# The row-maximum pass of pooled-query attention on full-height TensorE tiles

## The chip, the cores and the metric

The kernel runs on one core of a Trainium2 chip. The metric is the device time of one execution in microseconds; a run of the kernel before is given as the median of its executions. A profile of one execution shows what each engine did: TensorE (PE, with its weight loads as PEld), VectorE (DVE), ScalarE (ACT), GpSimd (POOL) and SyncE (SP), which issues all transfers here.

## The reference

The computation is an attention over 8 batches and 8 heads, with keys and values of 1152 rows of 64, whose queries are the means of neighbouring rows (576 per head), followed by a feed-forward block with g = h cos(h). The shapes of the feed-forward block are 4608 x 512 times 512 x 2048, and 2048 x 512 back.

```python
q_pool = q.reshape(B, H, S // 2, 2, D).mean(axis=3)
scores = scale * np.matmul(q_pool, k.transpose(0, 1, 3, 2))
scores = scores - np.max(scores, axis=-1, keepdims=True)
attn = np.exp(scores)
attn = attn / (np.sum(attn, axis=-1, keepdims=True) + 1e-09)
x = np.matmul(attn, v)            # then heads side by side: (4608, 512)
h = x @ w_in
out = (h * np.cos(h)) @ w_out
```

## The kernel before

**Precision.** Every f32 operand that is multiplied is split into a high and a low f16 half, and products are summed from three f16 matmuls. `q1T` holds the high half of the pooled queries, transposed and stacked twice (64 + 64 partitions); `k1` holds, per head, the high half of the keys in one half of the partitions and the low half in the other. `q2T` and `k2` hold the low half of the queries together with the row maxima, so that the score matmuls subtract the maximum by themselves.

**Pairs and units.** Two heads of a batch make a pair; there are 32 pairs. The 576 pooled queries of a head are four tiles of 128 and a remainder of 64; the remainders of the two heads share one slot (`2 * QT`) of the query tiles, head 0 in the first 64 rows and head 1 in the other. The main loop walks over 32 x 9 units: scores (`s_unit`, line 875, and `s_rem`, line 895), exponentials and their split into halves (`soft`, lines 921 to 930), the products with the values (`av`, line 945), and a share of the feed-forward block of an earlier batch (`ffn1`, line 1190, `ffn2`, line 1246).

**The row-maximum pass.** Before the exponentials of a pair, the pass finds the maximum of every score row. It is spread over the units of the two pairs ahead by the table `JOBS`, and each group writes a two-bank tile `mx` (one buffer, for the first pair alternating with `st`), from which VectorE takes the maxima:

- `mx_main` (line 670): eight groups per pair (four query tiles, two key chunks), each of two matmuls, one per head, of 64 contraction rows, 128 output rows and 512 columns;
- `mx_rest` (line 687, in the profile 688): one group of eight matmuls of 128 columns for the last 128 keys;
- `mx_mixed` (line 710): one group of four matmuls for the remainders, on 64 x 64 tiles, 512 columns;
- `mx_mixed_rest` (line 727): one group of two such matmuls of 128 columns.

The head's half of the partitions, `HALF[h]`, selects the tile rows, so the pass multiplies high halves with high halves only.

**Preparing the queries.** `pool_q` adds neighbouring rows on POOL, `prep_q1` writes the f16 copy twice into `q1s` (ScalarE for the first four pairs, VectorE behind them), `transpose_q1` transposes it by a DMA on SP's queue into `q1T`, and `prep_q2` forms the low half on POOL. `q1s` is a tile of a pool with one buffer.

**The order of work.** All instructions are recorded first, then `arrange` puts them into an order for each engine: a list schedule with a cost for each instruction, in which the earliest possible start wins. Its costs for TensorE are 0.421 ns per output column, nothing for a matmul on the lower half of a tile of 64 rows, and 0.1 us where the tile height changes:

```python
            if size[0] == 64 and tuple(i.tile_position)[0] == 64:
                c = 0.0
...
        if e == "PE" and nd["tile"] != mode:
            c += 0.1
            mode = nd["tile"]
```

The order within an engine is then fixed; semaphores hold an instruction back until its inputs are there.

Of the kernel before, what the change touches and what calls it, by code (L numbers as in the profile page):

```python
# [10 lines left out]
F16 = mybir.dt.float16  # L11
# [8 lines left out]
P = 128  # L20
# [19 lines left out]
NDIR = 4  # L40
# [277 lines left out]
def tile_attention_ffn(  # L318
# [9 lines left out]
    nc = tc.nc  # L328
    B, H, S, D = q.shape
# [11 lines left out]
    KT = S // P  # L341
    QT = SQ // P
# [8 lines left out]
    NSL = 2 * QT + 1  # L351
    RB = 512 // P
    JR = 2 * RB
    HALF = (slice(0, D), slice(D, P))

    fix = ctx.enter_context(tc.tile_pool(name="fix", bufs=1))
    sb1 = ctx.enter_context(tc.tile_pool(name="sb1", bufs=1))
# [4 lines left out]
    k2 = [fix.tile([P, KT, 2, P], F16, name=f"k2_{i}") for i in range(2)]  # L362
    qs2 = fix.tile([P, NSL, P], F16, name="qs2")
    nc.gpsimd.memset(qs2, 0.0)
    vc = [fix.tile([P, 2, KT, 2 * D + 2], F16, name=f"vc_{i}") for i in range(2)]
    vf = [t.bitcast(F32) for t in vc]
    for i in range(2):
# [193 lines left out]
    def after(ins, prev):  # L561
        if prev is not None:
            extra.append((ins.ins.name, prev.ins.name))
        return ins

    k1 = [fix.tile([P, KT, 2, P], F16, name=f"k1_{i}") for i in range(3)]
    kst, kld, qld, q1T, q2T, vld, vam, mxs = {}, {}, {}, {}, {}, {}, {}, {}
# [42 lines left out]

    def prep_q1(n):
        qs = qld[n][:, :, 0, :]
        q1s = sb1.tile([P, NSL, 2, D], F16, tag="q1s", name="q1s")
        src = qs.unsqueeze(2).broadcast_to([P, NSL, 2, D])
        if n < NDIR:
            nc.scalar.copy(q1s, src)
        else:
            nc.vector.tensor_copy(q1s, src)
        qld[n] = qs, q1s

    def transpose_q1(n):
        q1s = qld[n][1]
        t = sb1.tile([P, NSL, P], F16, tag="q1T", bufs=3, name="q1T")
        tr = nc.sync.dma_start_transpose(t, q1s.rearrange("p s a d -> p (s a d)"))
        if gate[0] is None:
            gate[0] = tr
        q1T[n] = t

    def prep_q2(n):
        qs, q1s = qld.pop(n)  # L630
        v4 = qs2[:, 0 : 2 * QT].rearrange("p (t h) (a d) -> p t (h a) d", h=2, a=2)
        nc.gpsimd.tensor_sub(
            v4[:, :, 0::3, :],
            qs[:, 0 : 2 * QT].rearrange("p (t h) d -> p t h d", h=2),
            q1s[:, 0 : 2 * QT, 0, :].rearrange("p (t h) d -> p t h d", h=2),
        )
        for h in range(2):
            nc.gpsimd.tensor_sub(
                qs2[HALF[h], 2 * QT, HALF[h]],
                qs[HALF[h], 2 * QT],  # L640
                q1s[HALF[h], 2 * QT, 0],
            )

    def transpose_k(n, js):
# [13 lines left out]
    def mx_tile(n):  # L658
        mx_n[0] += 1
        tag = "st" if n == 0 and mx_n[0] % 2 else "mx"  # L660
        return psum.tile([P, 2, 512], F32, tag=tag, name=tag)

    def mx_main(n, t, c):
        if n not in mxs:
            mxs[n] = sb2.tile([P, NSL, 3], F32, tag="mxs", name="mxs")
        m = mx_tile(n)
        last = None
        for h in range(2):
            last = after(
                nc.tensor.matmul(  # L670
                    m[:, h, :],
                    q1T[n][HALF[h], 2 * t + h, :],
                    k1[n % 3][HALF[h], c * RB : (c + 1) * RB, h, :],
                    start=True,
                    stop=True,
                    skip_group_check=True,
                ),
                last,
            )
        nc.vector.reduce_max(mxs[n][:, 2 * t : 2 * t + 2, c], m, axis=AX.X)  # L680

    def mx_rest(n):
        m = mx_tile(n)
        last = None
        for t in range(QT):
            for h in range(2):
                last = after(
                    nc.tensor.matmul(
                        m[:, h, t * P : (t + 1) * P],
                        q1T[n][HALF[h], 2 * t + h, :],  # L690
                        k1[n % 3][HALF[h], KT - 1, h, :],
                        start=True,
                        stop=True,
                        skip_group_check=True,
                    ),
                    last,
                )
        nc.vector.reduce_max(
            mxs[n][:, 0 : 2 * QT, 2].rearrange("p (t h) -> p h t", h=2),
            m.rearrange("p h (t c) -> p h t c", c=P),  # L700
            axis=AX.X,
        )

    def mx_mixed(n):
        m = mx_tile(n)
        last = None
        for c in range(2):
            for h in range(2):
                last = after(
                    nc.tensor.matmul(  # L710
                        m[HALF[h], (c + h) % 2, :],
                        q1T[n][HALF[h], 2 * QT, HALF[h]],
                        k1[n % 3][HALF[h], c * RB : (c + 1) * RB, h, :],
                        start=True,
                        stop=True,
                        skip_group_check=True,
                    ),
                    last,
                )
        nc.vector.reduce_max(mxs[n][:, 2 * QT, 0:2], m, axis=AX.X)  # L720

    def mx_mixed_rest(n):
        m = mx_tile(n)
        last = None
        for h in range(2):
            last = after(
                nc.tensor.matmul(
                    m[HALF[h], 0, 0:P],
                    q1T[n][HALF[h], 2 * QT, HALF[h]],
                    k1[n % 3][HALF[h], KT - 1, h, :],  # L730
                    start=True,
                    stop=True,
                    skip_group_check=True,
                ),
                last,
            )
        nc.vector.reduce_max(mxs[n][:, 2 * QT, 2:3], m[:, 0, 0:P], axis=AX.X)
# [78 lines left out]
    def mains(c, ts):  # L816
        def fn(n):
            for t in ts:
                mx_main(n, t, c)

        return fn
# [6 lines left out]
        (-2, 1, lambda n: transpose_k(n, J0)),  # L828
        (-2, 2, lambda n: load_k(n, J1)),
        (-2, 2, prep_q1),  # L830
        (-2, 2, transpose_q1),
        (-2, 3, lambda n: prep_k(n, J1)),
        (-2, 3, lambda n: transpose_k(n, J1)),
# [3 lines left out]
        (-2, 6, mains(0, (2,))),  # L837
        (-2, 7, mains(0, (3,))),
        (-2, 7, prep_q2),
        (-2, 8, mains(1, (0,))),  # L840
        (-2, 8, load_v),
# [3 lines left out]
        (-1, 0, v_max_begin),  # L845
        (-1, 1, mains(1, (3,))),
        (-1, 2, mx_rest),
        (-1, 2, mx_mixed),
        (-1, 3, mx_mixed_rest),
        (-1, 3, m_write),  # L850
        (-1, 4, transpose_q2),
# [13 lines left out]
    def s_unit(u):  # L865
        if u >= NP * NU:
            return
        p, i = divmod(u, NU)
        ka, kb, qa, qb = k1[p % 3], k2[p % 2], q1T[p], q2T[p]
        if i > 0:  # L870
            j = i - 1
            s = psum.tile([P, 2, 512], F32, tag="st", name="st")
            for h in range(2):
                for w, x, part in ((ka, qa, 0), (kb, qb, 1)):
                    nc.tensor.matmul(  # L875
                        s[:, h, :].rearrange("p (t c) -> p t c", c=P),
                        w[:, j, h, :],
                        x[:, h : 2 * QT : 2, :],
                        start=part == 0,
                        stop=part == 1,  # L880
                        skip_group_check=True,
                    )
            st[u] = [(s.rearrange("p a c -> p (a c)"), 2 * 512)]
            return
        st[u] = [s_rem(p, 0, JR, "st")]

    def s_rem(p, j0, j1, tag):
        ka, kb, qa, qb = k1[p % 3], k2[p % 2], q1T[p], q2T[p]
        s = psum.tile([P, 2, 512], F32, tag=tag, name=tag)
        for j in range(j0, j1):  # L890
            r = j - j0
            for h in range(2):
                for w, x, part in ((ka, qa, 0), (kb, qb, 1)):
                    o = (r % RB) * P + h * D
                    nc.tensor.matmul(  # L895
                        s[:, r // RB, o : o + D],
                        w[:, j, h, :],
                        x[:, 2 * QT, HALF[h]],
                        start=r % RB == 0 and h == 0 and part == 0,
                        stop=False,  # L900
                        skip_group_check=True,
                    )
        n = (j1 - j0) * P
        return s.rearrange("p a c -> p (a c)")[:, 0:n], n
# [478 lines left out]
    for u in range(NUNITS):  # L1383
# [10 lines left out]
        while credit > 0.0:  # L1394
            c = next(ffn, None)
# [47 lines left out]
```

## Time and profile before

| | us |
|---|---|
| three runs, median (lowest to highest) | 1680.79 (1677.89 to 1682.36) |
| profiled execution, span from first to last instruction | 1669.1 |
| profiled execution, own time | not given apart from the span |
| TensorE busy in it | 1554.3 |
| ScalarE busy | 1216.6 |
| VectorE busy | 1141.3 |
| POOL busy | 888.7 |

A busy time is the union of an engine's recorded instructions. Matmuls are pipelined: a matmul starts before the record of the one ahead ends, so recorded lengths add up to more than the time that TensorE spends, and the distance between starts is what a matmul costs in a stream. A shape like `64*128 64x512` names the part of the array in use (rows * columns), and then partitions x elements of the moving operand. The granted clock is the share of TensorE's full clock. The first row-maximum matmul starts at 17.1 us and the last at 1447.1 us; from 1517 us on the core works on the rest of the feed-forward block alone.

### The profile page before, as it was taken

The numbers are of one execution on the slowest core, as the hardware profiler recorded it, in microseconds if no ns is written. First come the engines' busy times: TensorE is split into PE (matmuls) and PEld (weight loads), VectorE is DVE, ScalarE is ACT, GpSimd is POOL, SyncE is SP. The second block draws the span as 40 slices with busy tenths as digits, with TensorE's granted clock in tenths as the row PEclk, the third lists the DMA queues.
The fourth block names the chain that finished last, engine by engine and source line by source line (L and its number), as shares of the span: only waits on it lengthen the run. The fifth ranks groups of instructions, "written<-read, shape, count | busy, mean of one in ns | idle before, by whom it ended". The sixth has DMA issues, their size and how long they took to land. (4 is left out here: it accounts for less than half of the span.)

```text
span 1669.1 us, 40505 instructions
## 1 busy us (share of the span) xinstructions
PE 1554.3 (93%) x17080; PEld 1015.9 (61%) x17080; DVE 1141.3 (68%) x1630; ACT 1216.6 (73%) x1476; POOL 888.7 (53%) x765
## 2 busy tenths in 40 slices
PE   3899998998899989998999999999999999997998
PEld 1577776665666566654666566665666566665664
DVE  6799896777667777766866577776678767632342
ACT  2346468887788779886987597988798879884442
POOL 3334255566566755665465556665665665461222
PEclk9899999999999999998999999999999999998999
DMA  9876853336415453444444225335434343101000
GB/s 222 188 175 137 154 103 64 79 87 111 93 49 123 79 108 67 102 79 84 90 86 97 69 51 114 65 88 98 104 78 101 63 109 52 28 21 27 14 26 19
DMA packets 336566, 146.31 MB, mean 88 GB/s; under 512 B 243712, under 2 KB 319488, under 8 KB 336384
## 3 DMA queue, kind: packets, MB, share of 16 engines
q1 hardware_dynamic: 336384, 143.73, 41.1%
q8 instruction: 133, 2.18, 0.6%
q14 instruction: 49, 0.40, 0.1%
HBM read 76.55 MB, written 10.50 MB: 52 GB/s over the span
## 5 line engine op out<-in xcount | busy, mean ns | idle before, releaser
L930 POOL TENSOR_TENSOR pp<-e,pp 128x512 f16<-128x512 f32 x374 | 445.9, 1214 | 298.8 <-ACT pp L924 126.3
L1190 PE MATMUL f<-xT,w 128*128 128x256 f16 x3456 | 416.8, 277 | 12.7 <-DVE y L1216 8.4
L921 ACT ACTIVATE e<-st,eb 128x1024 f32<-128x1024 f32 x280 | 311.1, 1111 | 137.9 <-PE st L875 100.4
L680 DVE TENSOR_REDUCE mxs<-mx 128x2 f32<-128x1024 f32 x252 | 307.5, 1220 | 151.2 <-PE mx L670 150.0
L1246 PE MATMUL f<-w,g 128*128 128x512 f16 x1728 | 395.6, 379 | 0.0
L1190 PEld LDWEIGHTS <-w 128*128 128x128 f16 x3456 | 331.6, 99 | 86.3 <-issue 37.3
L924 ACT CAST pp<-e 128x1024 f16<-128x1024 f32 x280 | 292.5, 1045 | 8.1
L945 PEld LDWEIGHTS <-pp 128*128 128x128 f16 (+1 forms) x7392 | 243.1, 100 | 76.4 <-POOL pp L930 22.7
L1246 PEld LDWEIGHTS <-g 128*128 128x128 f16 x1728 | 160.7, 98 | 192.7 <-issue 13.8
L1155 POOL TENSOR_TENSOR g<-hsc,g 128x512 f16<-128x512 f32 x144 | 188.9, 1337 | 154.8 <-ACT g L1154 145.8
L945 PE MATMUL ava<-vc,pp 128*128 128x64 f16 (+4 forms) x4784 | 249.8, 203 | 17.8 <-POOL pp L930 16.4
L875 PE MATMUL st<-q1T,k 128*128 128x512 f16 x576 | 223.0, 387 | 14.9 <-ACT e L921 14.1
L875 PE MATMUL st<-q2T,k 128*128 128x512 f16 x576 | 223.0, 387 | 0.0
L945 PE MATMUL avb<-vc,pp 128*128 128x65 f16 (+1 forms) x3312 | 206.8, 201 | 3.0 <-POOL pp L930 3.0
L1216 DVE SCALAR_TENSOR_TENSOR y<-f,r1a,y 128x512 f32<-128x512 f32 x144 | 106.9, 746 | 108.7 <-ACT y L1215 108.5
L875 PEld LDWEIGHTS <-k 128*128 128x128 f16 x1152 | 101.2, 99 | 101.9 <-issue 25.6
L1212 ACT ACTIVATE hsc<-f,r 128x512 f32<-128x512 f32 x144 | 98.3, 683 | 75.7 <-PE f L1190 74.0
L1145 DVE TENSOR_TENSOR hsc<-hsc,y 128x512 f32<-128x512 f32 x144 | 130.0, 951 | 34.2 <-ACT y L1139 33.7
L926 DVE TENSOR_TENSOR pp<-e,pp 128x1024 f16<-128x1024 f32 x93 | 128.5, 1381 | 35.3 <-ACT pp L924 34.5
L603 POOL TENSOR_TENSOR kst<-kld,kst 128x512 f16<-128x512 f32 x64 | 89.3, 1396 | 100.8 <-ACT kst L602 84.8
L670 PE MATMUL mx<-k,q1T 64*128 64x512 f16 x504 | 102.0, 401 | 33.3 <-DVE mxs L680 11.9
L670 PEld LDWEIGHTS <-q1T 64*128 64x128 f16 x512 | 26.1, 93 | 131.1 <-issue 102.8
(117 smaller groups left out, 1641.2 us busy)
## 6 DMA issues: line engine op xcount, KB each, us to landing
vld<-in_v_dram SPq DMA_DIRECT2D x32, 576.0 KB, 4.1
qld<-in_q_dram SPq DMA_DIRECT2D x64, 256.0 KB, 3.4
kld<-in_k_dram SPq DMA_DIRECT2D x32, 320.0 KB, 3.9
kld<-in_k_dram SPq DMA_DIRECT2D x32, 256.0 KB, 3.8
wraw<-in_moe_w_in_dram SPq DMA_DIRECT2D x8, 1024.0 KB, 6.5
wraw<-in_moe_w_out_dram SPq DMA_DIRECT2D x8, 1024.0 KB, 7.1
out_dram<-ob SPq DMA_DIRECT2D x32, 256.0 KB, 2.4
k<-k SPq DMA_DIRECT2D x64, 80.0 KB, 3.2
```

What stands on the lines that cost most here:

```text
L670: nc.tensor.matmul(m[:, h, :], q1T[n][HALF[h], 2 * t + h, :], k1[n % 3][HALF[h], c * RB : (c + 1) * RB, h, :], start=True, stop=True, skip ...
L680: nc.vector.reduce_max(mxs[n][:, 2 * t : 2 * t + 2, c], m, axis=AX.X)
L875: nc.tensor.matmul(s[:, h, :].rearrange("p (t c) -> p t c", c=P), w[:, j, h, :], x[:, h : 2 * QT : 2, :], start=part == 0, stop=part == 1, ...
L921: nc.scalar.activation(e, s, AF.Exp, scale=exp_scale, bias=eb)
L924: nc.scalar.copy(pp[:, 0], e)
L926: nc.vector.tensor_sub(pp[:, 1], e, pp[:, 0])
L930: nc.gpsimd.tensor_sub(pp[:, 1, c], e[:, c], pp[:, 0, c])
L945: mm = nc.tensor.matmul(out, w, x, start=start, stop=False, skip_group_check=True)
L1145: nc.vector.tensor_mul(hj, hj, y[:, j : j + 2])
L1155: nc.gpsimd.tensor_sub(gt[:, 1], hj, gt[:, 0])
L1190: mm = nc.tensor.matmul(ps[:, fi, :], w1[wt][:, hp, fs], ck.xT[hp][:, xi, cs], start=n == 0, stop=n == 3 * HP - 1, skip_group_check=True,)
L1246: nc.tensor.matmul(po, gt[:, gi, f % 2, ts_], w2[wt][:, f, :], start=f == 0 and (gi, wt) == (0, 0), stop=f == NF - 1 and (gi, wt) == (1, 0),)
```

## The change

The groups of the row-maximum pass use all 128 contraction rows. For the main and rest groups the same `q1T` slot (the query stacked twice) is multiplied by the whole `k1` slice, so that high and low halves of the keys are summed. For the remainders, the shared slot is split in two: slot `2 * QT` holds head 0's rows with zeros in the other 64, slot `2 * QT + 1` holds head 1's, and the two matmuls of a chunk are summed in one bank. `q1s` becomes a fixed tile of ten slots, of which the last two are zeroed once by POOL; `prep_q1` writes it in three copies (eight slots, then one half slot per head). `q1T` has ten slots, `s_rem` reads head 1's remainder from the last, and the transpose covers ten blocks. The scratch reserved for software-generated transfers is set to 1024 bytes. The reductions, the counts of matmuls and the job table stay.

```diff
+    q1s = fix.tile([P, NSL + 1, 2, D], F16, name="q1s")
+    nc.gpsimd.memset(q1s[:, 2 * QT :], 0.0)
...
     def prep_q1(n):
         qs = qld[n][:, :, 0, :]
-        q1s = sb1.tile([P, NSL, 2, D], F16, tag="q1s", name="q1s")
-        src = qs.unsqueeze(2).broadcast_to([P, NSL, 2, D])
-        if n < NDIR:
-            nc.scalar.copy(q1s, src)
-        else:
-            nc.vector.tensor_copy(q1s, src)
-        qld[n] = qs, q1s
+        parts = [(slice(0, P), slice(0, 2 * QT), slice(0, 2 * QT))]
+        for h in range(2):
+            parts.append((HALF[h], slice(2 * QT, NSL), slice(2 * QT + h, 2 * QT + h + 1)))
+        for ps, a, b in parts:
+            src = qs[ps, a]
+            src = src.unsqueeze(2).broadcast_to([src.shape[0], src.shape[1], 2, D])
+            if n < NDIR:
+                nc.scalar.copy(q1s[ps, b], src)
+            else:
+                nc.vector.tensor_copy(q1s[ps, b], src)
+        qld[n] = qs
...
-        t = sb1.tile([P, NSL, P], F16, tag="q1T", bufs=3, name="q1T")
+        t = sb1.tile([P, NSL + 1, P], F16, tag="q1T", bufs=3, name="q1T")
...
-                q1s[HALF[h], 2 * QT, 0],
+                q1s[HALF[h], 2 * QT + h, 0],
...
                     m[:, h, :],
-                    q1T[n][HALF[h], 2 * t + h, :],
-                    k1[n % 3][HALF[h], c * RB : (c + 1) * RB, h, :],
+                    q1T[n][:, 2 * t + h, :],
+                    k1[n % 3][:, c * RB : (c + 1) * RB, h, :],
...
                         m[:, h, t * P : (t + 1) * P],
-                        q1T[n][HALF[h], 2 * t + h, :],
-                        k1[n % 3][HALF[h], KT - 1, h, :],
+                        q1T[n][:, 2 * t + h, :],
+                        k1[n % 3][:, KT - 1, h, :],
...
-                        m[HALF[h], (c + h) % 2, :],
-                        q1T[n][HALF[h], 2 * QT, HALF[h]],
-                        k1[n % 3][HALF[h], c * RB : (c + 1) * RB, h, :],
-                        start=True,
-                        stop=True,
+                        m[:, c, :],
+                        q1T[n][:, 2 * QT + h, :],
+                        k1[n % 3][:, c * RB : (c + 1) * RB, h, :],
+                        start=h == 0,
+                        stop=h == 1,
...
-                    m[HALF[h], 0, 0:P],
-                    q1T[n][HALF[h], 2 * QT, HALF[h]],
-                    k1[n % 3][HALF[h], KT - 1, h, :],
-                    start=True,
-                    stop=True,
+                    m[:, 0, 0:P],
+                    q1T[n][:, 2 * QT + h, :],
+                    k1[n % 3][:, KT - 1, h, :],
+                    start=h == 0,
+                    stop=h == 1,
...
-                        x[:, 2 * QT, HALF[h]],
+                        x[:, 2 * QT + (h if part == 0 else 0), HALF[h]],
...
+        "TRN2", target_bir_lowering=False, num_devices=1, dynamic_dma_scratch_size=1024
```

More of the change, by code (lines that the diff above doesn't have):

```diff
@@ L612, in prep_q1 @@
         qs = qld[n][:, :, 0, :]
-        q1s = sb1.tile([P, NSL, 2, D], F16, tag="q1s", name="q1s")
-        src = qs.unsqueeze(2).broadcast_to([P, NSL, 2, D])
-        if n < NDIR:
-            nc.scalar.copy(q1s, src)
-        else:
-            nc.vector.tensor_copy(q1s, src)
-        qld[n] = qs, q1s
+        parts = [(slice(0, P), slice(0, 2 * QT), slice(0, 2 * QT))]
[9 more added lines that the diff above has]
+        qld[n] = qs
     def transpose_q1(n):
-        q1s = qld[n][1]
-        t = sb1.tile([P, NSL, P], F16, tag="q1T", bufs=3, name="q1T")
+        t = sb1.tile([P, NSL + 1, P], F16, tag="q1T", bufs=3, name="q1T")
         tr = nc.sync.dma_start_transpose(t, q1s.rearrange("p s a d -> p (s a d)"))
@@ L629, in prep_q2 @@
     def prep_q2(n):
-        qs, q1s = qld.pop(n)
+        qs = qld.pop(n)
         v4 = qs2[:, 0 : 2 * QT].rearrange("p (t h) (a d) -> p t (h a) d", h=2, a=2)
@@ L1422 @@
     from concourse.bass_utils import run_bass_kernel_spmd as _run
-    nc = _bacc.Bacc("TRN2", target_bir_lowering=False, num_devices=1)
+    nc = _bacc.Bacc(
+        "TRN2", target_bir_lowering=False, num_devices=1, dynamic_dma_scratch_size=1024
+    )
     arrays, args = {}, []
```

## The prediction

> **What bounds the kernel now.** I read the page's engine table first, then the table by stretches of the span, then the waits of TensorE, and last the timeline around single groups of the row-maximum pass.
>
> ```profile
> span 1669.1 us, 40505 instructions
> PE 1554.3 (93%) x17080; PEld 1015.9 (61%) x17080; DVE 1141.3 (68%) x1630; ACT 1216.6 (73%) x1476; POOL 888.7 (53%) x765
> 60.00:200.00 140.00, 131.52 (x1114) 100.63 (x1113) 119.85 (x198) 73.02 (x82) 51.58 (x33) 0.92 0.76 165
> 600.00:800.00 200.00, 190.06 (x2271) 121.76 (x2270) 146.65 (x212) 163.08 (x197) 121.09 (x108) 0.97 0.44 92
> 1200.00:1450.00 250.00, 245.88 (x2945) 157.28 (x2943) 183.67 (x270) 215.09 (x260) 151.78 (x134) 1.00 0.36 73
> PE st L670 <- DMA q1T<-q1s: 17.1, 1, 17.1
> PE ava L945 <- POOL pp L930: 16.4, 9, 6.9
> PE st L875 <- ACT e L921: 14.1, 12, 4.7
> PE mx L670 <- DVE mxs L680: 11.9, 11, 4.0
> ```
>
> In the stretches the columns are: length, then busy time of PE, PEld, DVE, ACT and POOL, then the granted clock. TensorE is busy 93% of the span; from 60 to 1450 us, where the row-maximum pass runs, it is idle 8.5 us of 140, 9.9 of 200 and 4.1 of 250 in the three rows shown. No other engine is above 87% in these rows. So TensorE's own stream sets the time, and the question is how much of that stream a row-maximum group takes before and after. Its busy time cannot answer that, because the recorded durations of pipelined matmuls overlap. I use starts: from the moment at which the matmul before the group has streamed out to the start of the first matmul behind the group.
>
> **The change part by part.** First the four kinds of group, at full clock. The timeline's columns are start, length, line, tiles, and count.
>
> ```profile
> 898.32 0.38 PE L875 MATMUL st<-q1T,k 128*128 128x512 f16 x1
> 898.54 0.38 PE L875 MATMUL st<-q2T,k 128*128 128x512 f16 x1
> 898.85 0.39 PE L670 MATMUL mx<-k,q1T 64*128 64x512 f16 x2
> 899.17 1.48 PE L1190 MATMUL f<-xT,w 128*128 128x256 f16 x12
> 900.49 0.41 PE L945 MATMUL ava<-vc,pp 128*128 128x65 f16 x8
> 900.74 0.41 PE L945 MATMUL avb<-vc,pp 128*128 128x65 f16 x8
> ...
> 923.61 2.75 PE L1246 MATMUL f<-w,g 128*128 128x512 f16 x12
> 926.30 0.39 PE L670 MATMUL mx<-k,q1T 64*128 64x512 f16 x2
> 926.62 5.35 PE L1246 MATMUL f<-w,g 128*128 128x512 f16 x24
> 931.81 1.47 PE L1190 MATMUL f<-xT,w 128*128 128x256 f16 x12
> ...
> 934.85 0.38 PE L875 MATMUL st<-q2T,k 128*128 128x512 f16 x1
> 935.16 0.40 PE L688 MATMUL mx<-k,q1T 64*128 64x128 f16 x8
> 935.49 1.49 PE L1190 MATMUL f<-xT,w 128*128 128x256 f16 x12
> 936.82 0.41 PE L945 MATMUL ava<-vc,pp 128*128 128x65 f16 x8
> 937.15 0.62 PE L710 MATMUL mx<-k,q1T 64*64 64x512 f16 x4
> 937.71 0.42 PE L945 MATMUL avb<-vc,pp 128*128 128x65 f16 x8
> ...
> 939.07 1.47 PE L1190 MATMUL f<-xT,w 128*128 128x256 f16 x12
> 940.47 0.24 PE L727 MATMUL mx<-k,q1T 64*64 64x128 f16 x2
> 940.65 1.49 PE L1190 MATMUL f<-xT,w 128*128 128x256 f16 x12
> ```
>
> Prices of a full-height matmul: 24 of 512 columns take 926.62 to 931.81, 0.216 us each; 12 of 256 columns take 899.17 to 900.49, 0.110 each; 8 of 64 or 65 columns take 900.49 to 900.74, 0.031 each. No f16 matmul of 128 columns on full height stands in the trace: its bounds are 0.031 and 0.110, and a straight line between them gives 0.057, which I take because the price runs nearly with the columns (0.110 to 0.216 from 256 to 512).
>
> Main groups (two matmuls of 64x512, eight groups per pair of heads). The matmul at 898.54 has streamed out at 898.756; the next stranger starts at 899.17: 0.414 us. The group behind the twelve of line 1246 gives 926.62 less (923.61 + 12 x 0.216), again 0.42. The two matmuls share the stretch (one row for both, 0.39 long, where two in turn would show 0.6), so it is one pass of 0.216 and 0.1 of dead time on either side. The neighbouring full-height kinds pass into one another without a gap (898.32 to 898.54, 900.49 to 900.74), so I put the dead time down to the change of tile size. After: 2 x 0.216 = 0.432 without dead time, **+0.018 per group**.
>
> Rest groups (eight of 64x128, one per pair): 935.49 less 935.066 is 0.424. After: 8 x 0.057 = 0.456, **+0.03** (bounds 0.25 to 0.88, so -0.18 to +0.46).
>
> Mixed groups (four of 64x512 on 64x64 tiles, one per pair): 937.71 less (936.82 + 8 x 0.031) is 0.64. After: four full passes, 0.864, **+0.22**. This is the dear one: the two diagonal tiles ran side by side, and now half of every pass multiplies zeros.
>
> Mixed rests (two of 64x128): 940.65 less (939.07 + 12 x 0.110) is 0.26. After: 2 x 0.057 = 0.114, **-0.15**: here two switches go and almost nothing comes.
>
> ```profile
> L670 PE MATMUL mx<-k,q1T 64*128 64x512 f16 x504 | 102.0, 401 | 33.3 <-DVE mxs L680 11.9 <-ACT es L921 7.8 <-ACT pps L916 7.6
> L688 PE MATMUL mx<-k,q1T 64*128 64x128 f16 x248 | 12.8, 224 | 2.5 <-DVE mxs L680 2.4
> L710 PE MATMUL mx<-k,q1T 64*64 64x512 f16 x128 | 21.1, 409 | 2.5 <-DVE mxs L698 2.0 <-DVE mxs L680 0.5
> L727 PE MATMUL mx<-k,q1T 64*64 64x128 f16 x62 | 7.5, 239 | 0.3 <-DVE mxs L720 0.2
> 949.16 0.58 PE L875 MATMUL st<-q1T,k 128*128 128x512 f16 x1 [2.95 <-ACT e L921]
> ...
> 950.39 0.63 PE L875 MATMUL st<-q2T,k 128*128 128x512 f16 x1
> 950.95 0.61 PE L670 MATMUL mx<-k,q1T 64*128 64x512 f16 x2
> 951.50 4.61 PE L1190 MATMUL f<-xT,w 128*128 128x256 f16 x24
> ```
>
> The counts give 32 pairs (128 mixed matmuls by four). For the 31 pairs behind the first: 248 x 0.018 = 4.5; 31 x 0.03 = 1.0; 31 x 0.22 = 6.8; 31 x -0.15 = -4.7. Together +7.6 us. In a half-clock stretch (matmuls of 512 columns 0.43 apart) a main group takes 0.68 (951.50 less 950.82) and would take 0.864, +0.18; with a granted clock of 0.92 to 1.00 that is some six groups, +1.0.
>
> [...]
>
> Query preparation (lines 611 to 619). One copy of 1152 elements becomes one of 1024 and two of 128.
>
> ```profile
> L618 DVE CAST q1s<-qld 128x1152 f16<-128x1152 f32 x28 | 37.7, 1345 | 32.5 <-POOL qld L609 32.4
> L924 ACT CAST pps<-es 128x128 f16<-128x128 f32 x28 | 8.3, 298 | 0.9
> 9.66 1.15 ACT L616 CAST q1s<-qld 128x1152 f16<-128x1152 f32 x1 [5.29 <-POOL qld L609]
> 10.84 1.32 SPq L624 DMA_TRANSPOSE q1T<-q1s  x1
> ```
>
> On VectorE: 1024/1152 of 1.345 is 1.20, plus 2 x 0.298 (the nearest row of that size, ScalarE's cast) is 1.79, so +0.45 for each of 28 pairs, 13 us of busy time on an engine with 528 us idle. I cost it at nothing: what waits for it is the transpose, and TensorE uses that one two units later. If the cover went, the bound is TensorE's 11.9 us of waits for reductions growing by 0.45 at each of its 11, +5. On ScalarE the first four pairs have 1.02 + 2 x 0.298 for 1.15, +0.47; for the first pair that delays TensorE's start at 17.1, which waits for this transpose. The transpose on SP's queue grows from nine blocks to ten: a ninth of the 1.32 us that its issue takes, +0.15; the loads queued behind it on SP move by as much and have units of slack. The startup thus gives +0.6; the first pairs' groups, paced there by the reductions, may add up to 11 x 0.2. I take +1 for the startup together.
>
> Priced at nothing: the memset of 256 elements (POOL's first wait, for ScalarE, outlasts it; uncovered, well under a microsecond); the column of the extra slot in lines 895 to 898 (same count and shapes); the smaller DMA scratch (the page's queues are the hardware and instruction ones; no row shows POOL issuing a transfer); the reductions, unchanged, though each starts up to 0.12 us later behind the longer group. The order of instructions is recomputed: the planner's cost of a main group goes from 0.416 with its two switches to 0.431, of a mixed one from 0.63 to 0.86, of a mixed rest from 0.25 to 0.11. These differ as the measured ones do, so the plan stays about as good, but its details will move.
>
> Cover: the added time falls partly into waits that TensorE has anyway, 22.5 us of the 590 in the three stretches, 3.8%. Bounds are nothing and all of it; I take a fifth off, since the waits are few and the extra is spread evenly: -2. Sum: 7.6 + 1.0 + 1.0 - 2 = **+7.6 us**. The profiled span would go from 1669.1 to about 1676.7. The page gives no time of its own for that execution beyond the span; the median of the runs, 1680.79, lies 11.7 above it, and I leave that margin alone: **1688.4 us**. A change of 0.3%, 5.0 us, is about what a measurement can tell from none.
>
> **The rivals.**
>
> Cover wins: the waits for POOL, ScalarE and reductions take up most of the extra, and their ends do not move. For it speaks that 3.8% of these 1390 us is some 53 us of waits, seven times the extra; against it, that POOL and ScalarE's work itself hangs on TensorE's scores and moves back with them. It leaves +0 to +5, about 1683.
>
> Faster, by stalls that the new order avoids. TensorE's longest single waits are 6.9 us for line 930's subtractions and 4.7 for line 921's exponentials, and the row at 949.16 shows what follows one of 2.95: the row of 24 matmuls of line 1190 then lasts 4.61 us in place of some 2.8, and with the matmuls between, about 3 us are lost to the half clock. The two longest gone would be -6.9 - 4.7 - 2 x 3 = -17.6, and with the +7.6 about 1671; one gone leaves the time about equal. It decides from two. Against it: nothing in the change aims at these waits.
>
> The same dice the other way: one new stall of that kind, about 1698.
>
> Narrow matmuls held up by their weight loads. If a matmul of 128 columns with a load of its own goes at the price of 256 columns, 0.110, the rest groups cost another 8 x 0.053 and the mixed rests 2 x 0.053: 31 x 0.53 is +16, 1705. Against it: matmuls of 64 columns with loads of their own run at 0.031. [...]
>
> The change does not do what it says: the dead time belongs to the change of operands, not of tile size, and stays. Then every group keeps 0.2 us: 341 x 0.2 = +68, 1756. The gapless passing of full-height kinds speaks against it.
>
> **How the numbers follow.** Forecast, slower by 5 to 11 us (1686 to 1692): 0.47. Cover wins, within 5 us: 0.28. Stalls avoided, faster: 0.16. A new stall: 0.06. Narrow matmuls: 0.02. Dead time stays: 0.01. So faster 0.16, same 0.28, slower 0.56. The range from 1675 to 1698 holds the forecast, the cover case, the small end of the avoided stalls and the new stall's centre; left out are most of the avoided stalls and the last two.
>
> **What would show it.** Main groups of two rows starting 0.216 apart, with no gap ahead and behind; mixed groups at 0.86; rest groups at 0.45; the mixed rest at 0.11; TensorE's idle time between 60 and 1450 us within some 10 us of now. It would be wrong if a gap of 0.1 us still stood at the groups' edges, if 128-column matmuls took more than 0.06, or if the long waits for lines 930 and 921 came in another number.

## The result, and the profile after

The changed kernel takes 1700.6 us (median) against 1679.34 for the kernel before on the same chip: ratio 1.0129, 95% interval 1.0104 to 1.0153, 21.3 us slower. The forecast was 1688.4, in a range of 1675 to 1698. The direction is right, the size is almost three times the forecast, and the time lies above the range. On a second chip the ratio is 1.0103 (1.0063 to 1.0143), 1710.6 against 1689.1. All times here are of undisturbed executions; one slow execution each of e4, of e12 and of the kernel before on the chip of e1 (2590 to 5050 us) is left out of the medians.

First the profile's page of the changed kernel (span, busy time of each engine), then, in its timeline, the four kinds of group. Line 675 is the main group, 693 the rest, 715 the mixed group, 732 the mixed rest.

```profile
span 1698.6 us, 40564 instructions
...
PE 1570.6 (92%) x17080; PEld 1070.4 (63%) x17080; DVE 1175.2 (69%) x1686; ACT 1217.3 (72%) x1484; POOL 903.5 (53%) x766
```

```profile
739.10 0.19 PE L900 MATMUL st<-q2T,k 128*128 128x64 f16 x1
739.12 0.59 PE L675 MATMUL mx<-k,q1T 128*128 128x512 f16 x2
739.56 2.78 PE L1195 MATMUL f<-xT,w 128*128 128x256 f16 x24
...
960.83 0.38 PE L880 MATMUL st<-q2T,k 128*128 128x512 f16 x1
961.05 0.61 PE L693 MATMUL mx<-k,q1T 128*128 128x128 f16 x8
961.50 1.47 PE L1195 MATMUL f<-xT,w 128*128 128x256 f16 x12
962.80 0.41 PE L950 MATMUL ava<-vc,pp 128*128 128x65 f16 x8
963.05 1.02 PE L715 MATMUL mx<-k,q1T 128*128 128x512 f16 x4
963.91 0.41 PE L950 MATMUL avb<-vc,pp 128*128 128x65 f16 x8
...
965.27 1.47 PE L1195 MATMUL f<-xT,w 128*128 128x256 f16 x12
966.58 0.27 PE L732 MATMUL mx<-k,q1T 128*128 128x128 f16 x2
966.69 1.47 PE L1195 MATMUL f<-xT,w 128*128 128x256 f16 x12
```

No group has a gap at its edges any more where it is shown: the main group starts 0.02 us behind a matmul of 64 columns and takes 739.12 to 739.56, 0.44; the rest 0.45, the mixed group 0.86, the mixed rest 0.11. So the price of each group is what was forecast, and the missing time is elsewhere. What changed beyond the forecast is VectorE's queue, at the copies of `prep_q1` (line 624). First the groups of that line, then one place in the timeline: VectorE, POOL and TensorE around a late copy, and the same three copies where POOL is idle.

```profile
L624 DVE CAST q1s<-qld 64x128 f16<-64x128 f32 x56 | 40.1, 715 | 0.9
...
L624 DVE CAST q1s<-qld 128x1024 f16<-128x1024 f32 x28 | 34.8, 1241 | 34.4 <-POOL qld L611 34.4
```

```profile
206.21 1.07 DVE L624 CAST q1s<-qld 128x1024 f16<-128x1024 f32 x3
...
643.29 4.95 POOL L935 TENSOR_TENSOR pp<-e,pp 128x512 f16<-128x512 f32 x4
...
643.37 3.85 DVE L624 CAST q1s<-qld 128x1024 f16<-128x1024 f32 x3 [6.35 <-POOL qld L611]
...
647.25 3.35 DVE L1150 TENSOR_TENSOR hsc<-hsc,y 128x512 f32<-128x512 f32 x4
...
650.51 1.22 DVE L685 TENSOR_REDUCE mxs<-mx 128x2 f32<-128x1024 f32 x1
...
651.78 0.21 PE L900 MATMUL mx<-q1T,k 128*128 128x64 f16 x1 [5.41 <-DVE mxs L685]
```

The three copies take 1.07 us together when POOL does nothing, and 3.85 beside POOL's subtractions. Per pair they average 2.67 (1.241 and twice 0.715). The single copy of nine slots of the kernel before took 1.345 on average, with 1.335 to 1.353 as extremes, wherever it stood; 20 of the 28 began beside a POOL instruction. So the new copies are a faster form that waits for POOL. Of the 28 large ones, 11 began while no POOL instruction ran and took 0.68 to 0.69; 17 began beside one, took 1.24 to 1.89, and each ended 0.55 behind that instruction's end. Of the 56 small ones, the 25 that began without POOL took 0.21 to 0.23; the 31 that began beside it took 0.38 to 1.42, and each ended 0.08 to 0.09 behind it. VectorE works its queue in the planned order; at 643.37 the copies had come late (6.35 us of waiting for POOL's sum of the queries), and behind them stood the products of line 1150 and the reduction that frees the `mx` buffer. TensorE waited 5.41 us for that buffer. Of this wait at most 2.5 us (3.85 less 1.345) can be the new copies': waiting for POOL's sum is as long in the kernel before, 32.4 us in all against 34.4 here.

### The profile page after: what moved, and what is told of

It is laid out like the page before. It is cut to its first block, busy times and chain, and to the rows that moved or that the text cites. A ratio compares the mean times of both kernels' runs of the same rounds, so it can differ in the third digit from the quotient of the medians.

```text
span 1698.6 us, 40564 instructions
## 1 busy us (share of the span) xinstructions
PE 1570.6 (92%) x17080; PEld 1070.4 (63%) x17080; DVE 1175.2 (69%) x1686; ACT 1217.3 (72%) x1484; POOL 903.5 (53%) x766
## 4 chain that ended last, share of the span: by engine, by line
PE 69%; DVE 10%; DMA 8%; ACT 6%; issue 3%; POOL 3%; SPq 2%; POOLq 0%; ACTq 0%; DVEq 0%
PE f L1251 20%; PE f L1195 16%; PE st L880 11%; PE ava L950 6%; PE avb L950 5%; PE mx L675 5%; DMA qld<-in_q_dram 4%; DVE mxs L685 2%; DVE q1s L624 2%; ACT e L926 2%; PE avb L1019 2%; PE mx L715 1%; DMA k<-kst 1%; POOL pp L935 1%; DMA xT<-xs 1%
## 5 line engine op out<-in xcount | busy, mean ns | idle before, releaser
L935 POOL TENSOR_TENSOR pp<-e,pp 128x512 f16<-128x512 f32 x374 | 453.2, 1234 | 303.9 <-ACT pp L929 155.2
L1195 PEld LDWEIGHTS <-w 128*128 128x128 f16 x3456 | 340.7, 99 | 88.8 <-issue 17.9
L950 PEld LDWEIGHTS <-pp 128*128 128x128 f16 (+1 forms) x7392 | 247.4, 100 | 69.0 <-POOL pp L935 14.5
L1251 PEld LDWEIGHTS <-g 128*128 128x128 f16 x1728 | 166.9, 98 | 193.0 <-issue 3.8
L1160 POOL TENSOR_TENSOR g<-hsc,g 128x512 f16<-128x512 f32 x144 | 194.3, 1374 | 148.5 <-ACT g L1159 140.9
L950 PE MATMUL ava<-vc,pp 128*128 128x64 f16 (+4 forms) x4784 | 245.1, 200 | 12.3 <-POOL pp L935 9.2
L675 PE MATMUL mx<-k,q1T 128*128 128x512 f16 x504 | 157.3, 395 | 25.3 <-DVE mxs L685 9.4
L931 DVE TENSOR_TENSOR pp<-e,pp 128x1024 f16<-128x1024 f32 x93 | 134.0, 1440 | 35.1 <-ACT pp L929 34.0
L675 PEld LDWEIGHTS <-q1T 128*128 128x128 f16 x512 | 47.9, 102 | 92.9 <-issue 36.0
```

The source lines that it names most:

```text
L675: nc.tensor.matmul(m[:, h, :], q1T[n][:, 2 * t + h, :], k1[n % 3][:, c * RB : (c + 1) * RB, h, :], start=True, stop=True, skip_group_check ...
L931: nc.vector.tensor_sub(pp[:, 1], e, pp[:, 0])
L935: nc.gpsimd.tensor_sub(pp[:, 1, c], e[:, c], pp[:, 0, c])
L950: mm = nc.tensor.matmul(out, w, x, start=start, stop=False, skip_group_check=True)
L1160: nc.gpsimd.tensor_sub(gt[:, 1], hj, gt[:, 0])
L1195: mm = nc.tensor.matmul(ps[:, fi, :], w1[wt][:, hp, fs], ck.xT[hp][:, xi, cs], start=n == 0, stop=n == 3 * HP - 1, skip_group_check=True,)
```

## The experiments

Every kernel was timed against the kernel before on its own chip (the medians of that one there: 1689 to 1693), so ratios are compared; where it matters, the kernels compared ran on one chip. Differences in us are between medians. The lines of code are shortened to what a switch does. Three switches describe nearly all of them. **Matmuls**: half height as before, or full. **Copies into `q1s`**: the single one of nine slots; the three of the change; or the same three made by reductions over one element, which give the same values:

```diff
-                nc.vector.tensor_copy(q1s[ps, b], src)
+                nc.vector.tensor_reduce(q1s[ps, b], src.unsqueeze(4), axis=AX.X, op=ALU.max)
```

**Order**: that of the changed kernel ("new"), or that of the kernel before ("old"), got by giving the planner the other kernel's costs for the row-maximum groups, the copies, the memset and the transpose:

```diff
+            if PLAN != "own" and i.name in REC:
+                as64 = PLAN == "before"
+                c = 0.0 if as64 and REC[i.name][1] else n_out(wr) * 0.000421
```

| run | matmuls | into q1s | order | median us | ratio (95%) |
|---|---|---|---|---|---|
| e1 | half | three copies | new | 1706.3 | 1.0095 (1.0068 to 1.0123) |
| e2 | full | three copies | nearly old | 1715.6 | 1.0167 (1.0140 to 1.0194) |
| e3 | full | three reductions | new | 1692.2 | 1.0018 (0.9992 to 1.0044) |
| e4 | half | three copies | nearly old | 1710.8 | 1.0130 (1.0096 to 1.0163) |
| e5 | full | three copies (the change) | new | 1710.6 | 1.0103 (1.0063 to 1.0143) |
| e6 | full | large copied, small reduced | new | 1698.2 | 1.0039 (1.0019 to 1.0058) |
| e7 | full | large reduced, small copied | new | 1707.9 | 1.0098 (1.0066 to 1.0130) |
| e9 | half | three reductions | nearly old | 1701.5 | 1.0059 (1.0032 to 1.0085) |
| e10 | full | three reductions | nearly old | 1706.6 | 1.0085 (1.0057 to 1.0113) |
| e11 | half, mixed rest full | three reductions | nearly old | 1697.5 | 1.0037 (1.0017 to 1.0058) |
| e12 | half | two copies | nearly old | 1705.1 | 1.0075 (1.0049 to 1.0102) |
| e13 | half | three reductions | old | 1706.3 | 1.0082 (1.0054 to 1.0110) |
| e14 | full | three reductions | old | 1705.3 | 1.0086 (1.0056 to 1.0116) |
| e15 | full | three copies | old | 1728.2 | 1.0221 (1.0185 to 1.0256) |
| e16 | half | two copies | old | 1706.8 | 1.0086 (1.0054 to 1.0118) |
| e17 | half | single copy, a reduction behind it | old | 1694.1 | 1.0012 (0.9991 to 1.0032) |
| e18 | half | single copy, on ScalarE | its own | 1675.6 | 0.9888 (0.9867 to 0.9909) |

e1 to e4 ran on one chip, e5 to e8 on a second, e9 to e12 on a third, e13 to e18 on a fourth. In the traces every engine of e1, e3, e5, e6 and e7 works in the order of the changed kernel, and in e13 to e17 in that of the kernel before, POOL's one memset aside.

**One part undone (e1 to e4).**

> The changed kernel with one thing undone: all matmuls of the row-maximum pass are again on 64-row and 64x64 tiles; the query preparation in three copies, the ten-slot transpose and the order of every engine stay those of the changed kernel. Kernel before 1679, changed kernel 1701. Theory PRICE (the full-height groups themselves cost some 8 us of TensorE time, the rest of the 21 us is something else): 1692 to 1694. Rival ALL-PE (the full-height matmuls cost all 21 us): 1680. Rival NOTHING (the matmuls are free, order and copies cost it all): 1700.

> The changed kernel, with the planner told the costs of the kernel before for the row-maximum groups, the query copies and the transpose, so that nearly every engine runs its instructions in the order of the kernel before. Theory PORT (the three copies into q1s run in a form that waits for POOL and stall VectorE's queue, in any order): 1697 to 1701. Rival ORDER (the new order is worse by some 13 us, the copies cost little): 1687 to 1689.

> The changed kernel in its own order, the three copies into q1s on VectorE replaced by maxima over one element, which give the same values. Theory PORT (a reduction does not wait for POOL, and each of the small ones takes about 0.3 us and not up to 1.2): 1688 to 1691, and the waits of TensorE for the mx buffer behind the reductions fall from 20 us to under 8. Rival ORDER: 1699 to 1701, waits as before.

> The kernel before in nearly its own order, with only the query preparation changed: three copies into the ten-slot q1s and a ten-block transpose. Theory PORT: 1689 to 1693. Rival ORDER: 1679 to 1682.

Taking the full-height matmuls away leaves most of the loss (e1, +17 us); taking the copies' waiting away leaves almost none of it (e3, +3 us, not told from nothing). The order of the kernel before does not rescue the change (e2, +27), and the copies alone slow the half-height kernel by 22 us there (e4). The expected times were reckoned from 1679, the kernel before on this chip takes 1689; counted from the kernel before, e1 lies between PRICE (+13 to +15) and NOTHING (+21), and e2, e3 and e4 all lie on PORT's side of ORDER. But none of the three is inside PORT's range: e2 +27 for +18 to +22, e3 +3 for +9 to +12, e4 +22 for +10 to +14. So PORT gives the direction and not the size. One detail of e3 missed too: the waits for the `mx` buffer were to fall from 20 us to under 8, and measured 16.4 in its profile. The rows of the kernel before, the changed kernel and e3 (us in total, times, longest):

```profile
PE mx L895 <- DVE mxs L680: 2.8, 2, 1.5
...
PE mx L900 <- DVE mxs L685: 20.1, 7, 5.4
...
PE mx L940 <- DVE mxs L725: 16.4, 7, 5.1
```

That wait belongs mostly to the new order, not to the copies; between the profiles of e5 and e3 no single kind of TensorE's waits differs by more than 4 us, so the gain is spread.

**Which copy (e5 to e8).** e6 and e7 replace the small ones or the large one by reductions; e8 is the kernel before, profiled again.

> The changed kernel once more, for a comparison on the same chip as the next two. Both theories: 1.3% slower than the kernel before, as it was.

> The changed kernel in its own order; only the two 64-row copies of each pair into q1s are made by VectorE reductions over one element, the copy of 1024 elements stays. Theory PORT-SMALL (the two small copies, 0.715 us each in the changed kernel against 0.28 for a reduction of their size, wait for POOL and hold VectorE's queue): most of the gain of replacing all three, 10 to 15 us below the changed kernel. Rival PORT-BIG (the copy of 1024, 0.68 us alone and up to 1.65 beside POOL, does it, mainly by blocking POOL): within 4 us of the changed kernel.

> The mirror of the run before it: only the copy of 1024 elements is made by a reduction, the two 64-row copies stay copies. PORT-SMALL: within 5 us of the changed kernel, and the small copies last 0.7 us on average again. PORT-BIG: 10 to 15 us below it.

> The kernel before, unchanged, for a second profile of it: its span and the start of TensorE. If the first profile's start at 17.1 us and span of 1669.1 us were those of a quick execution, this one starts at 20 to 22 us like the variants and lies 10 to 15 us above; if the ten-slot preparation causes the late start, it starts at 17 again.

The small ones: 12.4 us from e5 to e6, 2.7 from e5 to e7, the latter not told from nothing. The groups of VectorE in e5, e6 and e7, and the pages' spans and engine tables of e8, e5 and e6 in turn:

```profile
L663 DVE CAST q1s<-qld 64x128 f16<-64x128 f32 x56 | 40.1, 717 | 0.9
...
L663 DVE CAST q1s<-qld 128x1024 f16<-128x1024 f32 x28 | 34.7, 1240 | 38.9 <-POOL qld L639 38.9
```

```profile
L659 DVE TENSOR_REDUCE q1s<-qld 64x128 f16<-64x128 f32 x56 | 15.5, 276 | 0.9
```

```profile
L659 DVE TENSOR_REDUCE q1s<-qld 128x1024 f16<-128x1024 f32 x28 | 34.0, 1213 | 38.6 <-POOL qld L639 38.6
```

```profile
span 1689.7 us, 40505 instructions
...
PE 1560.0 (92%) x17080; PEld 1017.2 (60%) x17080; DVE 1145.9 (68%) x1630; ACT 1218.4 (72%) x1476; POOL 892.2 (53%) x765
```

```profile
span 1708.9 us, 40564 instructions
...
PE 1567.5 (92%) x17080; PEld 1068.1 (62%) x17080; DVE 1176.3 (69%) x1686; ACT 1219.4 (71%) x1484; POOL 903.5 (53%) x766
```

```profile
span 1687.8 us, 40564 instructions
...
PE 1560.6 (92%) x17080; PEld 1066.9 (63%) x17080; DVE 1149.6 (68%) x1686; ACT 1218.4 (72%) x1484; POOL 908.4 (54%) x766
```

By elements a copy of 128 should be the cheapest thing here; it lasts 0.717 us on average against 0.276 for the slower form, 25 us of VectorE's time over 56 of them. The large copy's average is the same in both forms. On one chip the profile of the change has 7.5 us more of TensorE's busy time and 11.7 us more of idle time than that of the kernel before (1708.9 less 1567.5, against 1689.7 less 1560.0). The 7.5 are not the price of the matmuls, near as they come to the forecast: with the same full-height matmuls and the same order, TensorE is busy 1560.6 us in e6 and 1575.1 in e7. In e6 the idle time is 127.2, no longer than before; but its profile is of its shortest execution (1689.6, median 1698.2), so the pages do not tell how the 12.4 us divide. e8 also corrects the baseline: TensorE starts at 20.5 us in it, and its span is 20.6 us above the first profile's, more than the 10 to 15 expected; some 10 of it is the chip (medians 1689.1 and 1679.3). The first profile was of a shorter execution than those timed (a span of 1669.1, times of 1676.5 and more), and most of the late start is not the change's: e5 starts at 21.8.

**The price of the matmuls, and one cost by itself (e9 to e12).** e11 sets the mixed rest alone to full height. e12 splits the single copy of the kernel before:

```diff
-        parts = [(slice(0, P), slice(0, NSL), slice(0, NSL))]
+        parts = [(slice(0, P), x, x) for x in (slice(0, 2 * QT), slice(2 * QT, NSL))]
```

> Matmuls on 64-row and 64x64 tiles as before, ten-slot preparation with all three copies made by reductions, order of nearly the kernel before. PORT: no copy waits for POOL any more, so within 5 us of the kernel before. Rival (the ten-slot preparation costs by its longer transpose or its third instruction, whatever its form): 10 us or more above it.

> The same kernel, order included, with the full-height matmuls; the difference to the run ahead is the price of the matmuls alone. By the prediction's terms 7.6 to 8.6 us without cover, 6 to 7 with it; if TensorE's waits cover most of it, 1 to 4.

> The same as the first of these, order included, with the two matmuls of 128 columns of the mixed rest alone at full height: 0.27 us in place of 0.11 for each of 32 pairs, so 3 to 5 us below that run, and perhaps below the kernel before. If a change of tile height costs nothing at places where TensorE waits anyway, no difference.

> The kernel before with one cost added by itself: its single copy of nine slots becomes one of eight and one of a single slot, with the same values, matmuls, transpose and nearly the same order. PORT: both copies now take the fast form that waits for POOL (the large one 0.68 us alone, the small one 0.2, up to 1.2 to 1.6 beside POOL), so 5 to 12 us slower than the kernel before, though VectorE has less to do by the elements. Rival (only the number or the 64-row shape of the copies matters): within 3 us.

Between e9 and e10 nothing differs but the matmuls: +5.1 us, somewhat under the 6 to 7 expected. e11 lies 4.0 below e9, in the range expected (its text has the two prices the wrong way round: 0.27 was before, 0.11 after), where the prediction's term was 4.7; the intervals of these pairs overlap, so each difference alone is not sure. e9 itself is a miss for PORT and a hit for its rival: 12 us above the kernel before with no copy on VectorE that waits for POOL (its reductions take 1.213 and 0.275 on average). And with that baseline e12's 15 us prove nothing, since its order was the same nearly old one. Small copies could there fall behind other work that became ready; the next runs tie the copies of a pair to one another in the planner, and then every engine has exactly the old order.

**In exactly the old order (e13 to e16).**

> Every engine in exactly the order of the kernel before; half-height matmuls; ten-slot preparation by three reductions. Theory START (the 10 us of the run like it came from the order of the first pairs, where its small copies could fall behind other work): within 4 us of the kernel before. Rival PREP (the ten-slot preparation costs 10 us in any form): 8 to 12 us above it.

> The same with full-height matmuls, in exactly the order of the kernel before: the price of the matmuls alone, 3 to 6 us above the run ahead after what the first two such pairs of runs showed (2.9 and 5.1); 7 to 8 by the prediction's terms.

> The change whole, copies included, in exactly the order of the kernel before. PORT: 12 to 15 us above the run ahead. If the new order of the changed kernel did part of the harm, this one lies below the changed kernel (21 above the kernel before); if the order did no harm, at or above it.

> The kernel before in exactly its own order, its one copy of nine slots split into eight and one. PORT (small copies in the fast form wait for POOL, 0.53 us each and one per pair here): 4 to 8 us above the kernel before, about half of what two small copies per pair cost. Rival (the 13 us of the run like it were the order of the first pairs): within 3 us.

START falls: with the order exactly equal the ten-slot preparation by reductions still costs 13.9 us, a little over PREP's 8 to 12. The matmuls cost nothing that can be told (e14 lies 1.0 below e13, where 3 to 6 above was expected). The copies cost 22.9 us against reductions in their place (e14 to e15), above the 12 to 15 expected and the clearest difference of the study. And the changed kernel in the old order is 36 us above the kernel before, against 21 in its own: the new order did not do harm, it gave back about 1%. The two copies of e16 cost 14 us, above the 4 to 8 expected, and no more than e13's reductions; so their time alone shows that the two are dearer than the one, not that the waiting for POOL makes it so. In the groups by form and TensorE's waits of e14, then e15:

```profile
L665 DVE TENSOR_REDUCE q1s<-qld 128x1024 f16<-128x1024 f32 x28 | 33.9, 1212 | 34.7 <-POOL qld L645 34.7
...
L665 DVE TENSOR_REDUCE q1s<-qld 64x128 f16<-64x128 f32 x56 | 15.4, 275 | 0.9
...
PE ava L999 <- POOL pp L984: 18.1, 8, 9.1
...
PE mx L764 <- DVE mxs L752: 4.7, 3, 3.0
```

```profile
L669 DVE CAST q1s<-qld 64x128 f16<-64x128 f32 x56 | 35.5, 634 | 0.9
...
L669 DVE CAST q1s<-qld 128x1024 f16<-128x1024 f32 x28 | 33.7, 1204 | 36.3 <-POOL qld L645 36.3
...
PE ava L999 <- POOL pp L984: 22.3, 9, 8.7
...
PE mx L764 <- DVE mxs L752: 13.7, 9, 4.3
```

With order and matmuls equal, TensorE waits 9 us longer for VectorE's reductions before its mixed groups (line 764) and 4 us longer for POOL's subtractions, by one profile of each. The first wait goes with the form of the copies: in the same order it is 11.8 us in e16, whose two copies are of the fast form (0.213 to 2.615 us in its trace), and 4.9 in e13, which has reductions; in the new order it is 8.8 in e5 and 5.7 in e3. So part of the copies' delay reaches TensorE through VectorE's queue, and e16 has a wait that e13 has not: their 14 us need not have one cause.

**The queue by itself, and a better version (e17, e18).**

> The kernel before in exactly its own order, with one reduction of 256 elements (about 0.4 us, its result unused) added to VectorE's queue right behind the copy into q1s, for 28 of the 32 pairs. The copy, the transpose and its time of issue stay, and a reduction does not wait for POOL. Theory QUEUE (0.4 us more in VectorE's queue at this place is paid by TensorE at most pairs): 8 to 14 us above the kernel before. Rival TRANSPOSE (the later or longer transpose of q1s made the 14 us of the run with reductions): within 3 us.

> A version that may beat both: the kernel before with the single copy into q1s on ScalarE for all pairs (1.15 us each there) and the plan made anew. If VectorE's queue is what is paid for, taking 1.35 us per pair from it gives 5 to 15 us, less what ScalarE's longer queue costs: 1675 to 1690 against 1690. If ScalarE's queue is as dear, no gain or a loss of up to 15.

The edit of e17, then that of e18:

```diff
+        if EXTRA and n >= NDIR:
+            ex = sb2.tile([P, 4], F32, tag="ex", name="ex")
+            x = nc.vector.tensor_reduce(ex, qs[:, 0:4], axis=AX.X, op=ALU.max)
```

```diff
-        if n < NDIR:
-            nc.scalar.copy(q1s, src)
-        else:
-            nc.vector.tensor_copy(q1s, src)
+        nc.scalar.copy(q1s, src)
```

The added reduction of e17 in the groups by form, and the page of e18:

```profile
L675 DVE TENSOR_REDUCE ex<-qld 128x4 f32<-128x256 f32 x28 | 11.4, 408 | 0.0
```

```profile
span 1675.1 us, 40498 instructions
...
PE 1551.9 (93%) x17080; PEld 1017.2 (61%) x17080; DVE 1114.9 (67%) x1602; ACT 1242.9 (74%) x1504; POOL 904.4 (54%) x765
```

The copy in its groups by form:

```profile
L664 ACT CAST q1s<-qld 128x1152 f16<-128x1152 f32 x32 | 36.7, 1148 | 37.3 <-POOL qld L646 37.3
```

QUEUE falls: 0.41 us more in VectorE's queue right behind the copy costs nothing that can be told (1.0012), on the chip and in the order in which e13 lost 13.9 us with about as much (1.21 + 2 x 0.275 = 1.76 for 1.345). What e13 has and e17 has not is that `q1s` is complete 0.4 us later and its transpose has ten blocks; e16 has the first without the second (VectorE is busy 1158.8 us there against 1145.9 in e8, 0.46 more for each of 28 pairs). That the lateness of the transpose is the cause would fit all three, but was not tried by itself, and stays open. The profiles show little of it directly: TensorE waits for `q1T` 23.0 us in e17, 26.8 in e13 and 25.2 in e16, each time in two waits, of which the first, before its start, is 18.0, 21.7 and 21.1. e13 and e16 also make several copies in place of one on ScalarE for the first four pairs, which e17 does not; that was not tried by itself either. So the 13.9 us of e13 stay unexplained. In the new order, planned for the longer preparation, the same three reductions with full-height matmuls cost 3 us (e3).

e18 beats both kernels: 1675.6 us, 1.1% below the kernel before. No copy into `q1s` is left on VectorE, the copy takes 1.148 in place of 1.345, and VectorE has 31 us less to do than in e8. Its granted clock is also higher, 0.976 to 0.983 over its runs against 0.969 to 0.975 for the kernel before on that chip. How much of the gain is the move, how much the new plan, and whether the clock is a cause or comes with fewer waits, was not separated.

## Why the prediction was wrong, by its own steps

- **What bounds the kernel.** Right in that TensorE is the busiest engine before and after (93% and 92%), but too narrow: the sum asked only what TensorE's own stream gains. Its idle time between 60 and 1450 us, which was to stay within some 10 us, grew from 60.2 to 76.3, and on one chip from 72.0 (e8) to 87.4 (e5); with the small copies reduced it is 72.7 (e6).
- **The four kinds of group.** Right, each within 0.02 us (0.44, 0.45, 0.86, 0.11), with the dead time gone at every place shown. Main, rest and mixed groups were dearer and the mixed rest cheaper, as said.
- **Their sum.** Too large where it can be tried: 5.1 us (e9 to e10), 4.8 (e4 to e2) and -1.0 (e13 to e14) with everything else equal, for a forecast of 8.6 less 2 of cover. Each is uncertain by some 5 us, their mean of 3 by less. The cover was probably larger than a fifth.
- **The query preparation: the step that failed.** "I cost it at nothing" is the term that was wrong. It rested on VectorE's idle time and on 0.298 us for a small copy, a price from ScalarE. On VectorE the small copy measured 0.715 (0.21 alone), because 31 of the 56 began beside a POOL instruction and ended only behind it (0.38 to 1.42), and the three of a pair together 2.67 in place of the 1.79 reckoned: +1.33 per pair, not +0.45. Nor did VectorE's idle time cover it. Against reductions in their place, the small copies alone cost 12.4 us in the new order and all three 22.9 in the old; in the new order the whole change without them is 3 us above the kernel before (e3), with them 21 (e5, on another chip). The bound given, +5, counted 0.45 us at each of 11 waits for reductions and was too low. The path is shown only in part: the waits for reductions before the mixed groups (4.7 to 13.7 us from e14 to e15).
- **The order.** "The plan stays about as good" was wrong the other way: planned anew, the change loses 1.0 to 1.3%; in the old order it loses 2.2%. Part of what the new order gains are the waits for POOL's subtractions, 22.3 us in e15 (old order) and 12.1 in e5 (new).
- **The startup**, +1, can't be told: TensorE's start varies by 3.4 us between two profiles of the kernel before, and is 1.3 us later in e5 than in e8.
- **The margin** of 11.7 us between span and median was not a margin: the second profile's execution took 1691.5 with a span of 1689.7. It did no harm, since the forecast was a difference.
- **The rivals.** None named VectorE's waiting for POOL. A new stall, at 1698, comes nearest in number, by luck: the loss sits in many waits. Cover wins saw rightly that the waits take up much of the matmuls' price. The stalls of line 930 did shrink (16.4 us over nine waits to 9.2 over six), but other waits outweighed that. The last two are refuted: a matmul of 128 columns with a load of its own takes 0.056 (0.45 over eight), not 0.110, and no gap stayed.

That the direction came out right owes little to the sum: the matmuls, which were to make the kernel slower, cost some 3 us, and the rest came from a term put at nothing.

## What to carry to other kernels

When one elementwise instruction becomes several, price each by a row of its own engine and form, and ask what it can be held up by; an engine that is idle a third of the time can still delay what stands behind a stalled instruction (4.7 against 13.7 us of waits from e14 to e15), though a short one may cost nothing (e17). A profile of before is one execution, and before two profiles are subtracted, the same kernel profiled twice on one chip tells what the difference is worth. Where the order of work comes from a planner, keep the order and change the instruction, then keep the instruction and change the order; here the copies lost time and the new order gave some back.

## What the runs showed of the hardware

The casts from f32 to f16 into `q1s` went at two speeds on VectorE. Of nine slots, 1152 elements, one took 1.345 us within 1% everywhere, 1.17 ns per element, beside POOL or not. Of eight slots it took 0.68 alone, 0.67 ns per element, and up to 1.89 beside POOL in the changed kernel; of one slot on 64 partitions 0.21 to 0.23 alone, up to 1.42 beside POOL, and 0.715 on average. The longest are 1.2 above the times alone, and one subtraction of POOL took 1.23 on average (line 935). POOL's own work ran longer there too: the 18 of these 128x512 subtractions that began during a copy of eight slots took 1.36 to 1.66, where the median of those beside no copy is 1.157. The reductions in the copies' place showed no such wait: 1.212 and 0.275 on average in e14, and none above 1.221 in e13, where POOL is busy 52% of the span. The trace records the nine-slot copy as 9 x 2 x 64 into a single run of 1152, that of eight slots as 8 x 2 x 64 into 1024, that of one slot as 2 x 64 into 128. What in these shapes makes the one form slower and free of POOL no run shows.

In the kernel before, a half-height group in a full-height stream had 0.1 us of dead time on either side (0.414 us for one pass of 0.216), and in the changed kernel the groups have none at the places shown, so two full-height matmuls of 512 columns in turn (0.44) took within 0.03 us as long as two half-height ones that ran side by side (0.41 to 0.42).
